# One 32-bit GpSimd addition that makes both pattern copies of a group, with a new order of the work

## The chip, the cores and the metric

The kernel runs on one core of one Trainium2 chip. The metric is the time of one execution in device microseconds. A time is given as the median of several runs. A profile shows one further execution, with every instruction of every engine: PE (TensorE), DVE (VectorE), ACT (ScalarE), POOL (GpSimd) and SP (SyncE, which issues most DMAs).

## The reference

Two independent attention blocks, A and B, each with S = 2048 tokens, D = 512 channels, 32 heads of 16 channels, in bfloat16. Block A is linear attention; block B is full softmax attention. Their outputs stand side by side in the result.

```python
# both: q, k, v = split((x @ wqkv)) into H = 32 heads of Dh = 16
# A
phi = lambda t: jnp.where(t > 0, t + 1, jnp.exp(t)) + 1e-6
kv = einsum("bhsd,bhse->bhde", phi(k), v); z = einsum("bhsd->bhd", phi(k))
o = einsum("bhqd,bhde->bhqe", phi(q), kv) / (einsum("bhqd,bhd->bhq", phi(q), z) + 1e-6)
a = merge_heads(o) @ wo
# B
p = softmax(einsum("bhqd,bhkd->bhqk", q, k) * Dh ** -0.5)
b = merge_heads(einsum("bhqk,bhkd->bhqd", p, v)) @ wo
return concatenate([a, b], axis=-1)
```

Most of the work is B's softmax: 32 heads x 2048 x 2048 scores, that is 2048 blocks of 128 keys by 512 queries.

## The kernel before, in words

**Blocks.** The scores of B are made transposed, in blocks of 128 keys (partitions) by 512 queries. A unit `u` is four heads and 512 queries; it has 16 x 4 = 64 blocks, and there are 32 units. For each block PE makes the scores (line 899: a matmul with 32 rows, four heads in the four row groups of the array), some engine makes the exponentials, and PE multiplies them by V with a column of ones (line 1306: 17 columns, four heads in the four column groups), summing into the one PSUM bank `pPV`. After a unit, DVE transposes the bank (line 1335), takes the reciprocal of the sums (line 1340), and POOL multiplies (line 1341).

**Two ways to an exponential.**
- ACT: one activation turns two or three blocks from the PSUM tile `pS` into f16 numbers in `PT` (line 1111).
- DVE and POOL: DVE scales a block from PSUM, adds a constant and writes it as a 16-bit integer into `DI` (line 1015). Read as f16, such a bit pattern is roughly the exponential, a straight line between powers of two. To make the error smaller, the sum of three patterns is used: the first, and two copies with a constant added to the integer (`SHIFT`, 328 and 656). PE multiplies each of the three by V: the first with `VX` (V scaled by `VW`), the two copies with `VV`. So such a block needs three PV matmuls and an ACT block one.

**Groups.** Two DVE blocks make a group (`DG = 2`), which lives in one of eight buffers of `DI` (`NDG = 8`). When both blocks are there, `chain` (line 1149) calls `shift` (line 1167) for copy 1 and copy 2. Each is either a POOL instruction (`on_pool`, lines 1174 to 1231) or, for copy 2 only and if POOL has much waiting (line 1239), a DVE instruction (`on_dve`, line 1170), which writes with a gap after every 32 numbers. In `DI` the eight first patterns stand together, then the eight copies 1, then the eight copies 2 (`di_at`). A POOL copy is a `tensor_scalar` on 16-bit integers, a multiplication by 1.0 and an addition. `on_pool` joins copies that are waiting: up to four copies of the same number from evenly spaced buffers in one instruction (line 1226), or one copy 1 and one copy 2 of different groups (line 1201; there copy 2 is made from copy 1).

**The order of the work** is planned in Python before anything runs. A list scheduler (lines 1575 to 1647) keeps a clock for each engine in `T` and candidates for each engine in `cands`, with a time at which they are ready, a priority and a price in us. It picks the earliest, and the run function of the pick emits instructions to that engine's queue. `Sched` turns reads and writes into semaphore waits. The prices are fixed: a POOL copy costs `PFX` = 0.272 us and 0.000834 us a pattern; `LPE["pool"]` (`PM` = -0.025) is the time from the end of a POOL instruction on that clock to its result being usable. `SEG` is a table with a row for each 12 us of PE's clock that sets 27 parameters of the planner, among them `PSH` and `DSH` (when DVE takes copy 2), `DBL` and `PBL` (how much may wait for DVE and POOL), `JN` (the longest join) and a seed for picks among near equals. So a change of a price or of a row reorders everything after it, and how many blocks go to ACT and how many to DVE comes out of the plan.

**Beside this** run block A (projections, line 609; `phi`, lines 721 to 724), B's projections and V (line 709 on DVE, and line 712 on POOL for `VX`), and the output projections, as jobs spread over the time.

Of the kernel before, what the change touches and what calls it, by code (L numbers as in the profile page):

```python
# [238 lines left out]
def bass_concat_heads__linear_attn_block__softmax_full_mha__prompt_kernel(nc, A_x, A_wqkv, A_wo, B_x, B_wqkv, B_wo, out):  # L239
# [89 lines left out]
    )  # L329
    GB = 0.0  # L330
    PM = -0.025
    JN = 4
    KSL = 0.02
    PFX = 0.272
# [33 lines left out]
    with es:  # L368
# [20 lines left out]

        def di_at(v, b):  # L390

            if v == 0:
                return b * (32 + DGW) + 32
            if v == 1:
                return NDG * (32 + DGW) + b * DGW
            return NDG * (32 + 2 * DGW) + b * ((DGW // 32) * 33 + 32)
# [120 lines left out]
        sch.add("pool", lambda e: e.memset(DI[:, 0:NDG * (32 + DGW)].rearrange("p (b n) -> p b n", b=NDG)[:, :, 0:32], 0.0), writes=[("DI", 2, b_) for b_ in range(NDG)])  # L517
        sch.add("pool", lambda e: e.memset(EA[:, 512:528], 0.0), writes=["EA"])
        for e_ in range(2):
            sch.add("dve", lambda e, e_=e_: e.tensor_reduce(PAR[:, e_:e_ + 1], ZMk[:].rearrange("p (a e) -> p e a", e=2)[:, e_, :],  # L520
                                                           axis=AX.X, op=ALU.max),
                    reads=["ZMk"], writes=[("PAR", e_)])
# [11 lines left out]
        LTO = {("pe", "dve"): 0.243, ("pe", "act"): 0.215, ("act", "dve"): 0.137, ("dve", "pool"): 0.166, ("pool", "dve"): -0.03, ("dve", "act"): 0.15}  # L534
# [165 lines left out]
        def v4_job(t4, Gp, **kw):  # L700
# [11 lines left out]
            st.append(("pool", 0.708, f_op("pool", lambda e: e.tensor_scalar(  # L712
# [436 lines left out]
        def chain(buf):  # L1149
# [17 lines left out]
            def shift(v, t_):  # L1167
                def on_dve(st_, en_):
                    wide = w + 32
                    sch.add("dve", lambda e: e.tensor_scalar(gapped(DI, di_at(v, buf), wide // 32, 32), DI[:, di_at(0, buf) - 32:di_at(0, buf) + w], 1.0, float(SHIFT[v - 1]),  # L1170
                                                             op0=ALU.mult, op1=ALU.add), reads=rk, writes=[("DI", v, buf)])
                    give(buf, v, "dve", en_)
# [71 lines left out]
            for v in (1, 2):  # L1244
                shift(v, s_["t"])
# [491 lines left out]
```

## Time and profile before

| | |
|---|---|
| median of 3 runs | 657.84 us (657.6 to 658.09) |
| the profiled execution's own time | 657.45 us |
| its span, first to last instruction | 655.7 us |
| chain that ended last, share of the span | DVE 45%, PE 32%, ACT 17%, POOL 3% |
| blocks on ACT, on DVE (PV matmuls from PT, from DI with VX) | 1355, 693 |
| pattern copies on POOL: instructions of lines 1226 and 1201 | 300 and 37 |
| pattern copies on DVE: instructions of line 1170 | 111 |

A row of a group of instructions has: line, engine, operation, output tile <- input tiles, shapes, count; then the busy time in us and the mean duration in ns; then the engine's idle time just before these instructions and what ended it. In the rows of stretches, each engine has its busy time and, in brackets, its number of instructions. Busy times of PE are modelled at their ends: a matmul of 512 columns shows 0.38 us though the next can follow sooner.

### The profile page before, as it was taken

Reading aid. Unit: us, or ns where it says so; the run is one execution under the profiler, and the core shown is the slowest. Engines: PE = TensorE matmul, PEld = TensorE weight load, DVE = VectorE, ACT = ScalarE, POOL = GpSimd, SP = SyncE. Lnnn points to the kernel's source line nnn. Section 1 sums busy time; section 2 is a strip of 40 time slices with the busy share of each in tenths; the row PEclk is TensorE's granted clock in tenths of the full one; section 3 lists DMA queues with packets and bytes.
Section 4 is the critical chain, followed back from the end, with each engine's and each line's share of the span. In section 5 each row is a group of like instructions: output and inputs, shape, how many; then the busy total and the mean of one; then the engine's idle time right before and its main releaser. Section 6 shows DMA issues by size and latency. Waiting matters only on the chain.

```text
span 655.7 us, 19281 instructions
## 1 busy us (share of the span) xinstructions
PE 639.1 (97%) x8321; PEld 215.3 (33%) x8322; DVE 633.4 (97%) x1101; ACT 641.4 (98%) x694; POOL 600.2 (92%) x418
## 2 busy tenths in 40 slices
PE   8999999999999999999999999999999999999995
PEld 5333433333333334322232223332323322232231
DVE  4999999999999999999999999999999999999984
ACT  6999999999999999999999999999999999999995
POOL 5999998999999999999999999999999999999994
PEclk9999999999999999999999999999999999999999
DMA  9701010111011103000210100100010010011111
GB/s 189 198 1 28 9 34 11 20 32 42 2 34 34 21 15 94 10 14 10 42 33 26 33 19 18 26 17 10 11 33 10 2 34 26 1 42 42 34 33 38
DMA packets 53227, 21.75 MB, mean 33 GB/s; under 512 B 44176, under 2 KB 52624, under 8 KB 53136
## 3 DMA queue, kind: packets, MB, share of 16 engines
q1 hardware_dynamic: 51664, 19.80, 13.2%
q8 instruction: 67, 1.10, 0.7%
q10 hardware_dynamic: 1472, 0.66, 0.4%
q14 instruction: 24, 0.20, 0.1%
HBM read 4.46 MB, written 4.19 MB: 13 GB/s over the span
## 4 chain that ended last, share of the span: by engine, by line
DVE 45%; PE 32%; ACT 17%; POOL 3%; DMA 1%; issue 1%; DVEq 0%; POOLq 0%
DVE DI L1015 30%; ACT PT L1111 17%; PE pPV L1306 11%; PE pS L899 11%; PE pD L609 6%; DVE DI L1170 5%; POOL DI L1226 2%; PE pS L609 2%; DVE OT L1335 1%; DVE KNa L724 1%; DVE VNa L764 1%; DVE VV L709 1%; DVE EC L722 1%; POOL DI L1201 1%; DMA xTb<-in_B_x_dram 1%
## 5 line engine op out<-in xcount | busy, mean ns | idle before, releaser
L1111 ACT ACTIVATE PT<-pS 128x1024 f16<-128x1024 f32 (+1 forms) x656 | 627.2, 1101 | 1.2 <-PE pS L899 1.0
L1226 POOL TENSOR_SCALAR DI<-DI 128x2048 int16<-128x2048 int16 (+2 forms) x300 | 491.6, 1639 | 33.7 <-DVE DI L1015 13.3
L1015 DVE TENSOR_SCALAR DI<-pD 128x512 int16<-128x512 f32 x505 | 330.6, 678 | 4.0 <-PE pD L899 2.4
L899 PE MATMUL pS<-QT,KM 32*128 32x512 bf16 x1543 | 260.4, 384 | 5.6 <-ACT PT L1111 4.7
L1306 PE MATMUL pPV<-PT,VV 128*17 128x512 f16 x1355 | 235.3, 381 | 0.0
L1306 PE MATMUL pPV<-DI,VV 128*17 128x512 f16 x1386 | 230.9, 383 | 0.7 <-DVE DI L1170 0.3
L899 PE MATMUL pD<-QT,KM 32*128 32x512 bf16 x505 | 181.2, 384 | 0.1
L1306 PE MATMUL pPV<-DI,VX 128*17 128x512 f16 x693 | 162.7, 381 | 0.7 <-DVE OT L1335 0.7
L899 PEld LDWEIGHTS pS<-QT,KM 32*128 32x128 bf16 x1543 | 65.2, 90 | 238.3 <-ACT PT L1111 183.8
L1015 DVE TENSOR_SCALAR DI<-pS 128x512 int16<-128x512 f32 x188 | 127.5, 678 | 0.1
L1170 DVE TENSOR_SCALAR DI<-DI 128x1056 int16<-128x1056 int16 x111 | 75.8, 690 | 0.3
L1201 POOL TENSOR_SCALAR DI<-DI 128x2048 int16<-128x2048 int16 x37 | 70.3, 1900 | 4.5 <-POOL DI L1226 1.8
L1306 PEld LDWEIGHTS pPV<-DI,VV 128*17 128x17 bf16 x1386 | 51.8, 88 | 50.2 <-issue 35.0
L1306 PEld LDWEIGHTS pPV<-PT,VV 128*17 128x17 bf16 x1355 | 53.9, 88 | 43.5 <-issue 32.0
L899 PEld LDWEIGHTS pD<-QT,KM 32*128 32x128 bf16 x505 | 43.4, 91 | 6.6 <-DVE DI L1015 4.6
L1306 PEld LDWEIGHTS pPV<-DI,VX 128*17 128x17 bf16 x693 | 37.1, 88 | 21.3 <-issue 13.0
L609 PE MATMUL pD<-Wa,xTa 128*32 128x256 bf16 x608 | 24.2, 275 | 0.3 <-DVE DI L1015 0.3
L609 PE MATMUL pD<-xTb,Wb 128*32 128x512 bf16 x304 | 23.9, 384 | 0.1
L1335 DVE STREAM_TRANSPOSE OT<-pPV 128x512 f32<-128x512 f32 x31 | 21.9, 706 | 0.0
L1341 POOL TENSOR_TENSOR OT<-OT,ZR 128x256 bf16<-128x256 f32 x31 | 19.3, 622 | 1.8
L609 PE MATMUL pS<-Wa,xTa 128*32 128x256 bf16 x416 | 16.9, 275 | 0.4 <-DVE DI L1015 0.4
L609 PEld LDWEIGHTS pD<-Wa,xTa 128*32 128x32 bf16 x608 | 13.2, 96 | 9.0 <-issue 5.3
(138 smaller groups left out, 384.9 us busy)
## 6 DMA issues: line engine op xcount, KB each, us to landing
out_dram<-KNa SPq DMA_DIRECT2D x31, 128.0 KB, 1.7
Wa<-in_A_wqkv_dram SPq DMA_DIRECT2D x1, 1536.0 KB, 8.3
KM<-KR SPq DMA_DIRECT2D x96, 16.0 KB, 1.8
Wb<-in_B_wqkv_dram SPq DMA_DIRECT2D x2, 384.0 KB, 4.8
Wb<-in_B_wqkv_dram SPq DMA_DIRECT2D x1, 512.0 KB, 4.7
Wa<-in_A_wo_dram SPq DMA_DIRECT2D x1, 512.0 KB, 4.6
Wa<-in_B_wo_dram SPq DMA_DIRECT2D x1, 512.0 KB, 4.4
ON<-in_B_x_dram ACTq DMA_DIRECT2D x1, 256.0 KB, 3.1
```

Source lines behind the costliest of these rows:

```text
L609: ins = self.e.matmul(out_[32 * g:32 * g + 32], lhsT=lhsT[:, 32 * g:32 * g + 32], rhs=rhs, start=start, stop=stop, tile_position=(0, 32 * g))
L709: st.append(("dve", 0.6, f_ev("dve", lambda e, bk: e.tensor_copy(VV[:, r, 4 * t4:4 * t4 + 4, :].rearrange("p t (h c) -> p t h c", c=17)[:, ...
L722: ("dve", 0.06 + n * 0.00054, f_op("dve", lambda e: e.tensor_scalar(gapped(EC, 0, n // 16 + 1, 16), EA[:, 0:n + 16], 1.0, 1e-6, op0=ALU.mi ...
L899: return e.matmul(dst, lhsT=KM[32 * g:32 * g + 32, Gp % 2, e_, j * 128:(j + 1) * 128], rhs=QT[32 * g:32 * g + 32, Gp % 2, c * 512:(c + 1) ...
L1015: sch.add("dve", lambda e: e.tensor_scalar(DI[:, di_at(0, buf) + i * 512:di_at(0, buf) + (i + n) * 512], f32v(DBANK[b0], n * 512), ESC, EB ...
L1111: sch.add("act", lambda e: e.activation(PTf[:, p0 * 512:p0 * 512 + w], S5[:, c0:c0 + w], ACTF.Exp, scale=SC), reads=skeys(sl, len(bl)), wr ...
L1170: sch.add("dve", lambda e: e.tensor_scalar(gapped(DI, di_at(v, buf), wide // 32, 32), DI[:, di_at(0, buf) - 32:di_at(0, buf) + w], 1.0, fl ...
L1201: sch.add("pool", lambda e: e.tensor_scalar(dv, sv, 1.0, float(SHIFT[0]), op0=ALU.mult, op1=ALU.add), reads=keys, writes=[("DI", v_, x) fo ...
L1226: sch.add("pool", lambda e: e.tensor_scalar(dv, sv, 1.0, sh_, op0=ALU.mult, op1=ALU.add), reads=keys, writes=[("DI", v, x) for x in best])
L1306: sch.add("pe", lambda e, g=g, j=j, c0=c0, V_=V_, r2=r2, P=P, first=first, last_=last_: e.matmul(PVb[32 * g:32 * g + 17, 0:512] if len(P.s ...
L1335: sch.add("dve", lambda e: e.transpose(OT[:, 0, :], PVb[:, 0:512]), reads=[("PV", g) for g in range(4)], writes=[("OT", 0)])
L1341: ("pool", 0.69, f_op("pool", lambda e: e.tensor_tensor(xn[:, :, 16 * e_:16 * e_ + 16], o[:, :, 0:16], zr.unsqueeze(2).broadcast_to([128, ...
```

## The change

Both copies of a group are made by one POOL `tensor_tensor` addition. `DI` is seen as 32-bit integers (`DW`), so one word holds two patterns; the other operand is a word of the new tile `CW`, whose two 16-bit halves both hold the number (328 in word 0, 656 in word 1), read again and again with step 0. The first patterns are read twice, with step 0 over the copies. For this the layout of `DI` changes: the first patterns, copy 1 and copy 2 of one buffer stand one after the other (`DIR` numbers a buffer). Where DVE makes copy 2, POOL's instruction makes copy 1 alone. Two neighbouring or evenly spaced groups can still be joined, as long as there are at most `JN` copies in all. The join of a copy 1 with another group's copy 2 is gone. The planner's prices change: `PFX`, `PM`, the latency from POOL to DVE, and the prices of two other POOL instructions. The rows of `SEG` are new.

```diff
-        (0.0,0.2,4,0.8,6,1,8,2,10.0,28,2.5,6.0,0.5,2.5,2,4.0,2.0,2.5,0.5,2,1,0.1,8,0,-9.0,4,2,6),
+        (0.0,0.3,4,5,0,0,8,2,9.5,36,2.5,6.0,1.8,1.8,2,7.0,2.0,3,1.5,1,1,0.1,4,0,-9.0,4,0.5,59),
...
-    PM = -0.025
+    PM = 0.097
-    PFX = 0.272
+    PFX = 0.144
...
+        DIR = 32 + 2 * DGW + (DGW // 32) * 33 + 32
+
         def di_at(v, b):
 
-            if v == 0:
-                return b * (32 + DGW) + 32
-            if v == 1:
-                return NDG * (32 + DGW) + b * DGW
-            return NDG * (32 + 2 * DGW) + b * ((DGW // 32) * 33 + 32)
+            return b * DIR + 32 + v * DGW
+        CW = sb("CW", [128, 2], mybir.dt.int32)
+        DW = DI.bitcast(mybir.dt.int32)
...
-        sch.add("pool", lambda e: e.memset(DI[:, 0:NDG * (32 + DGW)].rearrange("p (b n) -> p b n", b=NDG)[:, :, 0:32], 0.0), writes=[("DI", 2, b_) for b_ in range(NDG)])
+        sch.add("pool", lambda e: e.memset(DI[:, :].rearrange("p (b n) -> p b n", b=NDG)[:, :, 0:32], 0.0), writes=[("DI", 2, b_) for b_ in range(NDG)])
+        for v_ in range(2):
+            sch.add("pool", lambda e, v_=v_: e.memset(CW[:, v_:v_ + 1].bitcast(I16), float(SHIFT[v_])), writes=["CW"])
...
-        LTO = {("pe", "dve"): 0.243, ("pe", "act"): 0.215, ("act", "dve"): 0.137, ("dve", "pool"): 0.166, ("pool", "dve"): -0.03, ("dve", "act"): 0.15}
+        LTO = {("pe", "dve"): 0.243, ("pe", "act"): 0.215, ("act", "dve"): 0.137, ("dve", "pool"): 0.166, ("pool", "dve"): 0.07, ("dve", "act"): 0.15}
...
-            st.append(("pool", 0.708, f_op("pool", lambda e: e.tensor_scalar(
+            st.append(("pool", 0.61, f_op("pool", lambda e: e.tensor_scalar(
...
-            def shift(v, t_):
-                def on_dve(st_, en_):
...
-                def on_pool(st_, en_):
...
+            def on_pool(st_, en_):
+                near_ = {x[1]: x for x in pshift if x[0] == vs and x[2] == w and x[3][0] <= st_ + PMW}
+                near_[buf] = me[0]
+                best = [buf]
+                for step in range(1, NDG):
+                    run_ = [buf]
+                    while (len(run_) + 1) * len(vs) <= JN and run_[-1] + step in near_:
+                        run_.append(run_[-1] + step)
+                    while (len(run_) + 1) * len(vs) <= JN and run_[0] - step in near_:
+                        run_.insert(0, run_[0] - step)
+                    if len(run_) > len(best):
+                        best = run_
...
+                T["pool"] = en_ = st_ + PFX + len(best) * len(vs) * w * 0.000833
+                gs = [(best[1] - best[0]) * DIR // 2 if len(best) > 1 else 1, len(best)]
+                part = lambda t_: list(t_[:, 0:1].ap[0])
+                dv = bass.AP(DW, DW[:, di_at(vs[0], best[0]) // 2:].offset, [part(DW), gs, [DGW // 2, len(vs)], [1, w // 2]])
+                sv = bass.AP(DW, DW[:, di_at(0, best[0]) // 2:].offset, [part(DW), gs, [0, len(vs)], [1, w // 2]])
+                cv = bass.AP(CW, CW[:, vs[0] - 1:].offset, [part(CW), [0, len(best)], [1, len(vs)], [0, w // 2]])
+                sch.add("pool", lambda e: e.tensor_tensor(dv, sv, cv, op=ALU.add), reads=keys + ["CW"], writes=[("DI", v, x) for v in vs for x in best])
...
+            vs = (1, 2)
+            if late:
+                for v in vs:
+                    push("dve", s_["t"], -2, 0.06 + w * 0.00027, plain(v))
+                return
+            if p_backlog(s_["t"]) - DSH * d_backlog(s_["t"]) > PSH:
+                vs = (1,)
+                push("dve", s_["t"], 1, 0.06 + (w + 32) * 0.00053, on_dve)
+            for v in vs:
+                pv_give[buf, v] = lambda en_, v=v: give(buf, v, "pool", en_)
+            me = [(vs, buf, w, push("pool", s_["t"] + LTO["dve", "pool"], 0, PFX + len(vs) * w * 0.000833, on_pool), rk)]
+            pshift.append(me[0])
...
-                  ("pool", 0.69, f_op("pool", lambda e: e.tensor_tensor(xn[:, :, 16 * e_:16 * e_ + 16], o[:, :, 0:16],
+                  ("pool", 0.59, f_op("pool", lambda e: e.tensor_tensor(xn[:, :, 16 * e_:16 * e_ + 16], o[:, :, 0:16],
```

More of the change, by code (lines that the diff above doesn't have):

```diff
@@ L1165, in give @@
                     pv_ready[b[0]].append((en_ + (LPE["pool"] if lane == "pool" else LPE["dve"]), b, (P, ("DI", v, buf_)), ("d", buf_), "V"))
-            def shift(v, t_):
-                def on_dve(st_, en_):
[L1169 to L1172, printed above, removed]
-                def on_pool(st_, en_):
-                    near_ = {x[1]: x for x in pshift if x[0] == v and x[2] == w and x[3][0] <= st_ + PMW}
-                    best = [buf]
-                    for step in range(1, NDG):
-                        run_ = [buf]
-                        while len(run_) < JN and run_[-1] + step in near_:
-                            run_.append(run_[-1] + step)
-                        while len(run_) < JN and run_[0] - step in near_:
-                            run_.insert(0, run_[0] - step)
-                        if len(run_) > len(best):
-                            best = run_
-                    d1 = lambda b_: dgroup["st"][b_].get("v1", 1e9)
-                    two = [x for x in pshift if x[2] == w and x[1] != buf and x[0] != v and x[3][0] <= st_ + PMW
-                           and d1(x[1] if v == 1 else buf) <= st_]
-                    if len(best) == 1 and two:
-                        o = min(two, key=lambda x: x[3][2])
-                        pshift.remove(me[0])
-                        pshift.remove(o)
-                        cands["pool"].remove(o[3])
-                        segs = sorted([(buf, v), (o[1], o[0])])
-                        st_ = max(st_, o[3][0], d1(o[1] if v == 1 else buf) + 0.05)
-                        keys = []
-                        for b_, v_ in segs:
-                            keys += [("DI", 1, b_)] if v_ == 2 else [("DI", 0, b_, i) for i in range(n)]
-                        T["pool"] = en_ = st_ + PFX + 2 * w * 0.000834
-                        moves = sorted((di_at(v_ - 1, b_), di_at(v_, b_)) for b_, v_ in segs)
-                        sv, dv = [bass.AP(DI, DI[:, x[0]:x[0] + 1].offset, [list(DI[:, 0:w].ap[0]), [x[1] - x[0], 2], [1, w]]) for x in zip(*moves)]
-                        sch.add("pool", lambda e: e.tensor_scalar(dv, sv, 1.0, float(SHIFT[0]), op0=ALU.mult, op1=ALU.add),
-                                reads=keys, writes=[("DI", v_, x) for x, v_ in segs])
-                        for x, v_ in segs:
-                            if v_ == 1:
-                                dgroup["st"][x]["v1"] = en_
-                            pv_give[x, v_](en_)
-                        return
-                    keys = []
-                    for b_ in best:
-                        x = near_.get(b_, me[0])
-                        pshift.remove(x)
-                        if b_ != buf:
-                            cands["pool"].remove(x[3])
-                            st_ = max(st_, x[3][0])
-                        keys += [("DI", 0, b_, i) for i in range(n)]
-                    T["pool"] = en_ = st_ + PFX + len(best) * w * 0.000834
-                    moves = [(di_at(0, b_), di_at(v, b_)) for b_ in best]
-                    def view(offs):
-                        one = DI[:, offs[0]:offs[0] + w]
-                        if len(offs) == 1:
-                            return one
-                        return bass.AP(one.tensor, one.offset, [list(one.ap[0]), [offs[1] - offs[0], len(offs)], [1, w]])
-                    sv, dv = view([m_[0] for m_ in moves]), view([m_[1] for m_ in moves])
-                    sh_ = float(SHIFT[v - 1])
-                    sch.add("pool", lambda e: e.tensor_scalar(dv, sv, 1.0, sh_, op0=ALU.mult, op1=ALU.add),
-                            reads=keys, writes=[("DI", v, x) for x in best])
-                    for x in best:
-                        if v == 1:
-                            dgroup["st"][x]["v1"] = en_
-                        pv_give[x, v](en_)
-                pv_give[buf, v] = lambda en_: give(buf, v, "pool", en_)
-                if late:
-                    def plain(st_, en_):
-                        sch.add("dve", lambda e: e.tensor_scalar(DI[:, di_at(v, buf):di_at(v, buf) + w], DI[:, di_at(0, buf):di_at(0, buf) + w], 1.0, float(SHIFT[v - 1]), op0=ALU.mult, op1=ALU.add),
-                                reads=rk, writes=[("DI", v, buf)])
-                        give(buf, v, "plain", en_)
-                    push("dve", t_, -2, 0.06 + w * 0.00027, plain)
-                elif v == 2 and p_backlog(t_) - DSH * d_backlog(t_) > PSH:
-                    push("dve", t_, 1, 0.06 + (w + 32) * 0.00053, on_dve)
-                else:
-                    me = [(v, buf, w, push("pool", t_ + LTO["dve", "pool"], 0, PFX + w * 0.000834, on_pool), rk)]
-                    pshift.append(me[0])
@@ L1244, in chain, with on_dve, plain, run @@
-            for v in (1, 2):
-                shift(v, s_["t"])
+            def on_dve(st_, en_):
+                wide = w + 32
+                sch.add("dve", lambda e: e.tensor_scalar(gapped(DI, di_at(2, buf), wide // 32, 32), DI[:, di_at(0, buf) - 32:di_at(0, buf) + w], 1.0, float(SHIFT[1]),
+                                                         op0=ALU.mult, op1=ALU.add), reads=rk, writes=[("DI", 2, buf)])
+                give(buf, 2, "dve", en_)
+            def plain(v):
+                def run(st_, en_):
+                    sch.add("dve", lambda e: e.tensor_scalar(DI[:, di_at(v, buf):di_at(v, buf) + w], DI[:, di_at(0, buf):di_at(0, buf) + w], 1.0, float(SHIFT[v - 1]), op0=ALU.mult, op1=ALU.add),
+                            reads=rk, writes=[("DI", v, buf)])
+                    give(buf, v, "plain", en_)
+                return run
@@ new lines, in on_pool @@
+            def on_pool(st_, en_):
[10 more added lines that the diff above has]
+                        best = run_
+                keys = []
+                for b_ in best:
+                    x = near_[b_]
+                    pshift.remove(x)
+                    if b_ != buf:
+                        cands["pool"].remove(x[3])
+                        st_ = max(st_, x[3][0])
+                    keys += [("DI", 0, b_, i) for i in range(n)]
+                T["pool"] = en_ = st_ + PFX + len(best) * len(vs) * w * 0.000833
[5 more added lines that the diff above has]
+                sch.add("pool", lambda e: e.tensor_tensor(dv, sv, cv, op=ALU.add), reads=keys + ["CW"], writes=[("DI", v, x) for v in vs for x in best])
+                for x in best:
+                    for v in vs:
+                        pv_give[x, v](en_)
@@ new lines, in chain @@
+            vs = (1, 2)
[6 more added lines that the diff above has]
+                push("dve", s_["t"], 1, 0.06 + (w + 32) * 0.00053, on_dve)
+            for v in vs:
+                pv_give[buf, v] = lambda en_, v=v: give(buf, v, "pool", en_)
+            me = [(vs, buf, w, push("pool", s_["t"] + LTO["dve", "pool"], 0, PFX + len(vs) * w * 0.000833, on_pool), rk)]
```

106 rows, old and new, of the table SEG are left out of this document.

## The prediction

> **What bounds the kernel now.** I read the page first, then the busy time of three stretches (start, middle, end). Columns of the second fence: length of the stretch, then busy time and number of instructions of PE, PEld, DVE, ACT and POOL, granted clock, DMA share, GB/s.
>
> ```profile
> span 655.7 us, 19281 instructions
> PE 639.1 (97%) x8321; PEld 215.3 (33%) x8322; DVE 633.4 (97%) x1101; ACT 641.4 (98%) x694; POOL 600.2 (92%) x418
> ```
> ```profile
> 0.00:12.00 12.00, 9.45 (x105) 7.25 (x106) 4.99 (x15) 5.91 (x7) 7.72 (x27) 1.00 0.93 199
> 12.00:640.00 628.00, 620.24 (x8152) 205.28 (x8149) 621.34 (x1073) 627.80 (x681) 585.49 (x382) 1.00 0.13 30
> 640.00:656.00 16.00, 9.38 (x71) 2.81 (x72) 7.12 (x14) 7.66 (x9) 7.04 (x10) 0.91 0.13 38
> ```
>
> No single engine bounds it. In the middle 628 us ACT is busy for 627.80, so the span is start plus ACT's exponentials plus end: it gets shorter only if ACT has fewer blocks. PE has 7.76 us idle there, DVE 6.66. POOL shows 42.5 us idle, but part of that is not usable, as its rows show below. The granted clock is 1.00, so no term hangs on it.
>
> What passes between the engines is blocks of 128x512 scores. Next, the groups of instructions:
>
> ```profile
> L1111 ACT ACTIVATE PT<-pS 128x1024 f16<-128x1024 f32 (+1 forms) x656 | 627.2, 1101 | 1.2 <-PE pS L899 1.0
> L1306 PE MATMUL pPV<-PT,VV 128*17 128x512 f16 x1355 | 235.3, 381 | 0.0
> L1306 PE MATMUL pPV<-DI,VX 128*17 128x512 f16 x693 | 162.7, 381 | 0.7 <-DVE OT L1335 0.7
> ```
> ```profile
> L1015 DVE TENSOR_SCALAR DI<-pD 128x512 int16<-128x512 f32 x505 | 330.6, 678 | 4.0 <-PE pD L899 2.4 <-PE pS L899 0.7
> L1015 DVE TENSOR_SCALAR DI<-pS 128x512 int16<-128x512 f32 x188 | 127.5, 678 | 0.1
> L1170 DVE TENSOR_SCALAR DI<-DI 128x1056 int16<-128x1056 int16 x111 | 75.8, 690 | 0.3
> ```
>
> 1355 blocks have one PV matmul from PT: ACT made them. 693 have one from DI with VX: DVE made them; 2048 together. An ACT block costs ACT 627.2 / 1355 = 0.463 us. A DVE block costs DVE (330.6 + 127.5) / 693 = 0.661 us, two more PV matmuls on PE (three patterns instead of one), and two pattern copies. Two blocks make a group, so a copy of a group is 1024 patterns, and there are as many such copies as blocks, 693: DVE makes 111 of them (L1170, 0.690 us each), POOL the other 582.
>
> **POOL, before.** Its groups by shape, its longest waits, and two places of its timeline (start, duration):
>
> ```profile
> L1226 POOL TENSOR_SCALAR DI<-DI 128x2048 int16<-128x2048 int16 x177 | 336.4, 1901 | 20.3 <-DVE DI L1015 9.0
> L1226 POOL TENSOR_SCALAR DI<-DI 128x1024 int16<-128x1024 int16 x105 | 109.9, 1047 | 11.3 <-DVE DI L1015 3.7
> L1201 POOL TENSOR_SCALAR DI<-DI 128x2048 int16<-128x2048 int16 x37 | 70.3, 1900 | 4.5 <-POOL DI L1226 1.8 <-DVE DI L1015 0.6 <-DVE VNa L764 0.2
> L1226 POOL TENSOR_SCALAR DI<-DI 128x3072 int16<-128x3072 int16 x16 | 44.1, 2753 | 2.0 <-DVE DI L1015 0.6 <-DVE RHA L774 0.3
> L1341 POOL TENSOR_TENSOR OT<-OT,ZR 128x256 bf16<-128x256 f32 x31 | 19.3, 622 | 1.8
> L1226 POOL TENSOR_SCALAR DI<-DI 128x512 int16<-128x512 int16 x2 | 1.2, 621 | 0.2
> L1398 POOL TENSOR_TENSOR OT<-OT,ZR 128x128 bf16<-128x128 f32 x2 | 0.8, 402 | 0.9 <-DVE ZR L1397 0.9
> L518 POOL MEMSET EA<- 128x16 bf16 x1 | 0.1, 112 | 0.0
> ```
> ```profile
> POOL DI L1226 <- DVE DI L1015: 13.3, 35, 1.4
> POOL VX L712 <- DVE VV L709: 5.5, 4, 4.2
> ```
> ```profile
> 316.72 0.62 POOL L1341 TENSOR_TENSOR OT<-OT,ZR 128x256 bf16<-128x256 f32 x1
> 317.41 12.07 POOL L1226 TENSOR_SCALAR DI<-DI 128x2048 int16<-128x2048 int16 x7
> ...
> 336.70 0.62 POOL L1341 TENSOR_TENSOR OT<-OT,ZR 128x256 bf16<-128x256 f32 x1
> 337.29 3.88 POOL L1226 TENSOR_SCALAR DI<-DI 128x2048 int16<-128x2048 int16 x2
> ```
>
> From 1024 to 2048 patterns the duration rises by 854 ns, from 2048 to 3072 by 852: 0.834 ns a pattern and 193 ns fixed. Two in a row take 3.88 us, that is 2 x 1.90 and 0.08 between them. So an instruction occupies POOL for 0.272 us plus 0.854 a copy: 337 x 0.272 + 582 x 0.854 = 91.7 + 497.0 = 588.7 us. All the rest of POOL (other work, start, end, waits, of which the two rows above are 18.8) is 655.7 - 588.7 = 67 us.
>
> **What the change removes and adds on POOL.** The 337 TENSOR_SCALAR go; each group gets one TENSOR_TENSOR on 32-bit words, for both copies, or for one where DVE takes the other. Two groups can still be joined (four copies at most). For 582 copies that is between 146 instructions (always four) and 346 (one a group, no joins); I take 300, since joins need neighbouring buffers to be ready together, and before they reached only 582 / 337 = 1.7 copies.
>
> The price of one is not in the trace; the nearest rows are the TENSOR_TENSOR with a broadcast operand, L1341 and L1398. From 128 to 256 elements they rise by 220 ns: 1.72 ns an element, 182 ns fixed. A word carries two patterns, so a pattern would cost 0.86 ns, against 0.834: the word form wins nothing by size. Lower bound: 0.834 ns a pattern, the row of the one-input form. Upper bound: L1341 with no fixed share at all, 622 / 256 = 2.43 ns a word. I take the slope halfway between 0.834 and 0.86, 0.867 us a copy, since both rows nearly agree.
>
> The Trainium skill ("GPSIMD Engine Reference", section 3.1) speaks against the change here: it gives a two-input add on GpSimd about 2.6 cycles an element against about one for one input, and 4497 ns for 2048 of 32 bits, 2.2 ns an element. By that, a copy would cost 512 x 2.2 = 1.13 us (an estimate from that page). L1341 with 1.72 ns stands between, nearer to the change's side; no row has 32-bit integers.
>
> So the gain must come from the fixed part. It has two bounds: L1341 at 336.70 ends at 337.32 and its successor starts at 337.29, 0.03 earlier; the one at 316.72 ends at 317.34 and its successor starts at 317.41, 0.07 later. So 0.182 becomes 0.15 or 0.25 us an instruction. I take 0.15, because a TENSOR_TENSOR has both kinds of successor and the new planner prices (0.144, and 0.59 for L1341) put the order on the early one; the late one is a rival. For the same 582 copies: 300 x 0.15 + 582 x 0.867 = 45 + 505 = 550 us, 39 less than 588.7. Bounds: 70 if every end is the good one (146 x 0.15 + 497 = 519), 2 with the late handoff and 0.88 us a copy (75 + 512 = 587).
>
> **What 39 us of POOL are worth.** The new order has to turn them into fewer ACT blocks. For 1 us less of the span:
> - ACT must lose 1 / 0.463 = 2.16 blocks.
> - DVE must make them (2.16 x 0.661 = 1.43) and be 1 us shorter too: 2.43 us, which is 2.43 / 0.690 = 3.5 copies handed to POOL.
> - POOL takes 3.5 + 2.16 copies of 0.94 us (0.867 and half of 0.15), and is 1 us shorter: 6.3 us.
> So POOL allows 39 / 6.3 = 6.2 us. PE is asked for 2.16 x 2 more matmuls. Its pieces in the chain of work (start, duration):
>
> ```profile
> 308.20 0.55 PE pPV L1306 x8
> 315.40 0.76 PE pPV L1306 x12
> 322.43 0.97 PE pPV L1306 x16
> ```
> ```profile
> 120.00:180.00 60.00, 59.95 (x917) 21.36 (x909) 59.79 (x107) 60.00 (x67) 55.84 (x35) 1.00 0.14 26
> PE pPV L1306 <- POOL DI L1226: 0.2, 1, 0.2
> ```
>
> Four more matmuls cost 0.21 us, so 4.3 cost 0.23: each microsecond gained asks PE for 1.23. It has 7.76 us idle in the middle; the stretch 120 to 180 shows that idle can sink to 0.05 in 60, so some 0.5 stays: (7.76 - 0.5) / 1.23 = 5.9 us. PE binds a little before POOL; I take 5.9. DVE then makes 13 blocks more (706), POOL 616 copies, and L1170 falls by 21 to about 90.
>
> **Terms at nothing.** The two memsets of the constant and the zeroing over all rows: L518 costs 0.11 us, ahead of the first scores in a stretch where POOL is busy 7.72 of 12; uncovered they would cost 0.3. The new layout of DI moves no work. The first copy of a group now comes with the second, at 1.9 us instead of 1.05: behind it stand PV matmuls, which the order does last; before, PE stood idle for POOL's copies once, for 0.2 us. If that cover were gone, at most the 0.85 us would show, at the end of the work, where it cannot be reordered; POOL's next instruction waits for nothing new, since the copies of a group had the same inputs before. The DVE plain copies at the end have no row before; none is expected.
>
> **Sum.** The profiled execution took 657.45 us, its span 655.7, so 1.75 lie around it; the median of the three runs shown is 657.84, 0.4 above it. 657.45 - 5.9 = 651.55, and by the median 651.9: I say 652.
>
> **Rivals.**
> - *PE pays less than I think* (faster still). Both copies of a group arrive together, which fills rounds of four better: 1386 + 693 matmuls in full rounds of 0.21. If PE gives way, POOL's upper end is the limit, 70 / 6.3 = 11 us: 646 to 649. For: POOL's idle; against: PE's 59.95 of 60. Chance 0.14.
> - *The freed POOL time isn't converted* (no change). ACT is already at 627.80 of 628 and PE near full; if PE's idle is the price of changing between kinds of matmul, more DVE blocks only press on PE and 0 to 1.3 us are won: 656.5 to 659. Chance 0.12.
> - *The late handoff* (slower). If the word addition is followed 0.07 us late, as at 316.72, the fixed part is 0.25 and the order, laid out for 0.15, sends POOL 616 copies: 616 x 0.867 + 300 x 0.25 = 609; with the 67 of the rest and the 1.75 around the span 678, and with the 18.8 of waits gone 659. In the middle 668. It decides from a fixed part of about 0.24 us on (534 + 300 x 0.24 + 67 - 18.8 = 654, next to the span of 655.7). For: the one-input instructions all stand 0.08 apart; against: 336.70. Chance 0.10.
> - *The word costs more* (much slower). At L1341's upper bound, 2.43 ns, 616 copies of 512 words cost 766 us, and with the 67 of the rest the span would be 833. As the 1.72 ns row stands against it, chance 0.04. By the 2.2 ns of the Trainium skill ("GPSIMD Engine Reference", section 3.1) it would be about 800, an estimate from that page.
> That the order does not do what it says (two copies an instruction) is not possible by the diff: the second copy has no other path but L1170's.
>
> **How the numbers follow.** My forecast (649 to 656.5, 652 the likeliest) has 0.60; with the first rival faster is 0.74. A run of this kernel can be told from no change at about 0.2%, 1.3 us. Same 0.12, slower 0.14. The range goes from 646 (the first rival's end) to 660, past no change; it leaves out the two costly rivals but for their near end, and a little below.
>
> **What would show it.** In the profile after: a POOL TENSOR_TENSOR group DI<-DI,CW whose 2048 patterns (1024 words) take 1.85 to 1.95 us; its successor starting at its end or before; some 300 of them against 337; L1170 near 90; DVE blocks (VX matmuls) near 706; ACT's L1111 near 621 us; PE idle in the middle near 1 us. I am wrong if the word form takes over 2.1 us for 2048 patterns, if successors stand 0.07 apart, or if PE's idle stays near 8 us with POOL clearly under 90%.

## The result, and the profile after

The kernel after takes 651.27 us (median of 4 runs, 650.7 to 651.69) against 657.82 us (4 runs, 657.6 to 658.09): a ratio of 0.990, 95% interval 0.9883 to 0.9917. That is 6.55 us less; 5.9 were forecast. The profiled execution took 651.69 us, its span 649.9.

From the page and its three stretches (columns as before):

```profile
span 649.9 us, 19218 instructions
PE 637.8 (98%) x8355; PEld 214.4 (33%) x8356; DVE 622.5 (96%) x1080; ACT 633.5 (97%) x689; POOL 616.8 (95%) x347
ACT 66%; PE 16%; DVE 16%; DMA 1%; issue 0%; SPq 0%
```
```profile
0.00:12.00 12.00, 9.71 (x97) 7.45 (x98) 4.99 (x15) 5.45 (x7) 7.79 (x29) 1.00 0.87 189
12.00:640.00 628.00, 623.20 (x8227) 204.97 (x8228) 613.64 (x1056) 626.88 (x681) 608.23 (x316) 1.00 0.13 30
640.00:656.00 16.00, 4.94 (x43) 2.01 (x32) 3.89 (x9) 1.19 (x2) 0.81 (x2) 0.89 0.16 54
```

In the middle ACT is as full as before, 626.88 of 628 us; POOL is busier (608.23 us, before 585.49), and DVE is idle for 14.36 us, before 6.66. The gain stands in the last stretch, which ends 5.8 us sooner, because ACT had less to do in all. The third line of the page is the chain that ended last: two thirds of it are ACT now. The blocks:

```profile
L1113 ACT ACTIVATE PT<-pS 128x1024 f16<-128x1024 f32 (+1 forms) x651 | 619.4, 1096 | 1.9 <-PE pS L901 1.0
L1284 PE MATMUL pPV<-PT,VV 128*17 128x512 f16 x1338 | 232.6, 381 | 0.0
L1284 PE MATMUL pPV<-DI,VX 128*17 128x512 f16 x710 | 162.8, 381 | 0.4 <-DVE OT L1313 0.4
```
```profile
L1171 DVE TENSOR_SCALAR DI<-DI 128x1056 int16<-128x1056 int16 x73 | 49.8, 687 | 0.2
L1177 DVE TENSOR_SCALAR DI<-DI 128x1024 int16<-128x1024 int16 x4 | 1.5, 424 | 0.1
```

17 blocks went from ACT to DVE (1355 to 1338, 693 to 710), and 38 copies from DVE to POOL (111 to 73). Four more copies are made by DVE in a plain form (L1177), which the kernel before did not use. POOL by shape, and two places of its timeline:

```profile
L1208 POOL TENSOR_TENSOR DI<-DI,CW 128x2048 int32<-128x2048 int32 x79 | 283.4, 3600 | 1.7 <-DVE DI L1017 0.5
L1208 POOL TENSOR_TENSOR DI<-DI,CW 128x1024 int32<-128x1024 int32 x132 | 246.9, 1892 | 4.1 <-DVE DI L1017 3.8
L1208 POOL TENSOR_TENSOR DI<-DI,CW 128x512 int32<-128x512 int32 x53 | 55.0, 1039 | 0.0
```
```profile
314.92 0.62 POOL L1319 TENSOR_TENSOR OT<-OT,ZR 128x256 bf16<-128x256 f32 x1
315.50 17.26 POOL L1208 TENSOR_TENSOR DI<-DI,CW 128x2048 int32<-128x2048 int32 x7
...
324.60 8.15 POOL L1208 TENSOR_TENSOR DI<-DI,CW 128x2048 int32<-128x2048 int32 x3
332.71 0.62 POOL L1319 TENSOR_TENSOR OT<-OT,ZR 128x256 bf16<-128x256 f32 x1
333.30 1.04 POOL L1208 TENSOR_TENSOR DI<-DI,CW 128x512 int32<-128x512 int32 x1
```

264 instructions carry 79 x 4 + 132 x 2 + 53 = 633 copies. From 1024 to 2048 words the duration rises by 1708 ns, 1.668 ns a word, so a copy of 512 words costs 0.854 us as before, and 0.184 us is fixed. A successor that waits for nothing starts 0.04 us before its predecessor's end (314.92 + 0.62 against 315.50; 324.60 + 8.15 against 332.71). So an instruction occupies POOL for 0.142 us plus 0.854 a copy: 264 x 0.142 + 633 x 0.854 = 37 + 541 = 578 us, 10 less than the 588.7 of before for 51 copies more. The rest of POOL is 649.9 - 578 = 72 us.

### The profile page after: what moved, and what is told of

Its sections match the earlier page's. It is cut to its first block, busy times and chain, and to the rows that moved or that the text cites. A ratio compares the mean times of both kernels' runs of the same rounds, so it can differ in the third digit from the quotient of the medians.

```text
span 649.9 us, 19218 instructions
## 1 busy us (share of the span) xinstructions
PE 637.8 (98%) x8355; PEld 214.4 (33%) x8356; DVE 622.5 (96%) x1080; ACT 633.5 (97%) x689; POOL 616.8 (95%) x347
## 3 DMA queue, kind: packets, MB, share of 16 engines
q1 hardware_dynamic: 51664, 19.80, 13.3%
## 4 chain that ended last, share of the span: by engine, by line
ACT 66%; PE 16%; DVE 16%; DMA 1%; issue 0%; SPq 0%
ACT PT L1113 65%; DVE DI L1017 11%; PE pPV L1284 5%; PE pS L901 5%; PE pD L611 2%; ACT EA L723 1%; PE pS L611 1%; DVE DI L1171 1%; DMA xTb<-in_B_x_dram 1%; DVE PQT L726 1%; DVE VNa L813 1%; DVE KNa L597 0%; DVE OT L1313 0%; PE pS L1336 0%; PE pD L901 0%; DMA KNa<-VNa 0%
## 5 line engine op out<-in xcount | busy, mean ns | idle before, releaser
L1113 ACT ACTIVATE PT<-pS 128x1024 f16<-128x1024 f32 (+1 forms) x651 | 619.4, 1096 | 1.9 <-PE pS L901 1.0
L1208 POOL TENSOR_TENSOR DI<-DI,CW 128x1024 int32<-128x1024 int32 (+2 forms) x264 | 580.7, 2232 | 5.8 <-DVE DI L1017 4.3
L1017 DVE TENSOR_SCALAR DI<-pD 128x512 int16<-128x512 f32 x512 | 336.9, 682 | 5.7 <-PE pD L901 3.9
L1284 PE MATMUL pPV<-PT,VV 128*17 128x512 f16 x1338 | 232.6, 381 | 0.0
L901 PE MATMUL pD<-QT,KM 32*128 32x512 bf16 x516 | 185.7, 384 | 0.5 <-DVE DI L1017 0.4
L1017 DVE TENSOR_SCALAR DI<-pS 128x512 int16<-128x512 f32 x194 | 131.5, 678 | 0.3 <-PE pS L901 0.3
L1284 PEld LDWEIGHTS pPV<-DI,VV 128*17 128x17 bf16 x1420 | 49.5, 88 | 45.0 <-issue 33.6
L1171 DVE TENSOR_SCALAR DI<-DI 128x1056 int16<-128x1056 int16 x73 | 49.8, 687 | 0.2
L597 DVE CAST KNa<-pD 128x512 bf16<-128x512 f32 x21 | 14.3, 681 | 3.1 <-PE pD L611 3.1
L714 POOL TENSOR_SCALAR VX<-VV 128x544 bf16<-128x544 bf16 x16 | 10.2, 646 | 6.5 <-DVE VV L711 6.5
```

Of the source, the lines that this page charges most:

```text
L597: return lambda e, bk: (e.tensor_copy(out_fn(), in_fn(bk)) if lane == "dve" else e.activation(out_fn(), in_fn(bk), ACTF.Copy))
L714: st.append(("pool", 0.61, f_op("pool", lambda e: e.tensor_scalar(VX[:, r, 4 * t4:4 * t4 + 4, :].rearrange("p t c -> p (t c)"), VV[:, r, 4 ...
L901: return e.matmul(dst, lhsT=KM[32 * g:32 * g + 32, Gp % 2, e_, j * 128:(j + 1) * 128], rhs=QT[32 * g:32 * g + 32, Gp % 2, c * 512:(c + 1) ...
L1017: sch.add("dve", lambda e: e.tensor_scalar(DI[:, di_at(0, buf) + i * 512:di_at(0, buf) + (i + n) * 512], f32v(DBANK[b0], n * 512), ESC, EB ...
L1113: sch.add("act", lambda e: e.activation(PTf[:, p0 * 512:p0 * 512 + w], S5[:, c0:c0 + w], ACTF.Exp, scale=SC), reads=skeys(sl, len(bl)), wr ...
L1171: sch.add("dve", lambda e: e.tensor_scalar(gapped(DI, di_at(2, buf), wide // 32, 32), DI[:, di_at(0, buf) - 32:di_at(0, buf) + w], 1.0, fl ...
```

## The experiments

A handoff is the gap from the end of one POOL instruction to the start of the next. I call it late at 0.06 to 0.08 us and early at about -0.04.

My theory: a copy costs the same, the fixed part falls, POOL is thereby able to take more, and the new order turns this into fewer ACT blocks. Rivals: the order alone made the gain; POOL's time was spare; and the early handoff comes from the new layout of DI, not from the instruction.

**The layout alone** (layout16), the kernel before with

```diff
+        DIR = 32 + 2 * DGW + (DGW // 32) * 33 + 32
...
-            if v == 0:
-                return b * (32 + DGW) + 32
-            if v == 1:
-                return NDG * (32 + DGW) + b * DGW
-            return NDG * (32 + 2 * DGW) + b * ((DGW // 32) * 33 + 32)
+            return b * DIR + 32 + v * DGW
...
```

> The kernel before with one edit: DI laid out as in the kernel after (first patterns, copy 1 and copy 2 of a buffer one behind the other). Same order, same 16-bit additions. Theory place (the late handoff of 0.08 us comes from where copy 1 stands): the successors of the copies start 0.03 to 0.04 us early instead of 0.08 late, so 337 instructions give back about 40 us of POOL; the order is the old one, so POOL only waits longer for DVE (13 us before) and the time stays between 656 and 658. Theory kind (the late handoff belongs to the 16-bit TENSOR_SCALAR): handoffs stay at 0.08 and nothing changes, 657.8.

Measured: 657.75 us against 657.77, ratio 0.9996 (0.9986 to 1.0006). Its POOL timeline still has 3.88 us for two of 1.90:

```profile
367.96 3.88 POOL L1224 TENSOR_SCALAR DI<-DI 128x2048 int16<-128x2048 int16 x2 [0.52 <-DVE DI L1013]
```

The late handoff stays: it is not the place.

**The word addition with the copies elsewhere** (sep), the kernel after with

```diff
-            return b * DIR + 32 + v * DGW
+            return b * (32 + DGW) + 32 if v == 0 else NDG * (32 + DGW) + b * DIC + (v - 1) * DGW
...
```

> The kernel after with one edit: the first patterns stand in a region of their own, the two copies of a buffer in pairs behind it. Same order, same word additions. Theory place: handoffs become late (0.07 instead of -0.04), 264 x 0.11 = 29 us more of POOL, which has 20 us idle in the middle: slower, 655 to 670. Theory kind: handoffs stay early, 651.3 as after.

Measured: 651.77 us, ratio to the kernel before 0.9908 (0.9892 to 0.9925).

```profile
314.67 0.62 POOL L1320 TENSOR_TENSOR OT<-OT,ZR 128x256 bf16<-128x256 f32 x1
315.25 17.25 POOL L1209 TENSOR_TENSOR DI<-DI,CW 128x2048 int32<-128x2048 int32 x7
332.46 0.62 POOL L1320 TENSOR_TENSOR OT<-OT,ZR 128x256 bf16<-128x256 f32 x1
```

The handoffs stay early (314.67 + 0.62 against 315.25; 315.25 + 17.25 against 332.46), save where POOL waits for something. Place is ruled out from both sides.

**The new order with 16-bit additions** (two16), the kernel after with

```diff
-                sch.add("pool", lambda e: e.tensor_tensor(dv, sv, cv, op=ALU.add), reads=keys + ["CW"], ...)
+                for v in vs:
+                    sch.add("pool", lambda e, d16=d16, s16=s16, v=v: e.tensor_scalar(d16, s16, 1.0, float(SHIFT[v - 1]), op0=ALU.mult, op1=ALU.add), ...)
```

> The kernel after, same order and layout, but each word addition is replaced by 16-bit TENSOR_SCALAR additions, one for each copy number (joined groups stay joined): 264 + 211 = 475 instructions for the same 633 copies. My theory (a copy costs 0.854 us either way, the gain is the fixed part): theory place gives 475 x 0.15 + 541 = 612 us of POOL against 578 after; with the other 72 of POOL less up to 22 of waits the span is 662 to 684. Theory kind gives 475 x 0.272 + 541 = 670, a span of 720 to 742. Rival (POOL is not what limits, the order alone made the gain): under 655.

Measured: 730.95 us (one run), span 729.2. Its chain and POOL groups:

```profile
POOL 60%; DVE 20%; PE 15%; issue 4%; ACT 1%; DMA 1%; DVEq 0%
L1212 POOL TENSOR_SCALAR DI<-DI 128x2048 int16<-128x2048 int16 x168 | 318.8, 1898 | 13.3
L1212 POOL TENSOR_SCALAR DI<-DI 128x1024 int16<-128x1024 int16 x297 | 310.3, 1045 | 24.4 <-DVE DI L1017 1.4
PE pPV L1289 <- POOL DI L1212: 38.5, 64, 1.6
```

There are 465 additions, not the 475 expected, because ten of the joined instructions hold the copy 1 of two groups and no copy 2. The durations by size are the old ones. There are only more instructions, 0.06 to 0.08 us lie between any two additions, and PE now waits 38.5 us for copies. So the new order does not pay with the old instruction as it was, with 328 and 656.

**A little more of the fixed part** (pad), the kernel after with

```diff
...
+                sch.add("pool", lambda e: e.memset(PD[:, pd, :], 0.0), writes=[("PD", pd)])
                 sch.add("pool", lambda e: e.tensor_tensor(dv, sv, cv, op=ALU.add), ...)
```

> The kernel after with a small memset of a spare tile ahead of each of the 264 word additions, worth about 0.095 us of POOL each, 25 us in all: it brings the fixed part of 0.142 us near 0.24, the point from which the late handoff was to decide. Mine: POOL's sum is 578 + 25 + 72 = 675 less up to 22 of waits: span 653 to 675, about 660. Rival (the freed POOL time is spare, ACT alone limits): 651 to 652.

Measured: 669.71 us (669.21 to 671.1), ratio to the kernel before 1.0186 (1.0169 to 1.0203); span 667.4. Stretch, chain, wait and timeline:

```profile
12.00:640.00 628.00, 613.00 (x7973) 198.69 (x7969) 605.30 (x1032) 614.46 (x666) 622.41 (x569) 1.00 0.12 28
POOL 86%; PE 8%; DVE 4%; DMA 1%; ACT 0%; issue 0%
POOL DI L1213 <- DVE DI L1019: 2.7, 4, 1.3
...
304.14 1.90 POOL L1213 TENSOR_TENSOR DI<-DI,CW 128x1024 int32<-128x1024 int32 x1
305.97 0.16 POOL L1212 MEMSET PD<- 128x64 bf16 x1
306.07 1.90 POOL L1213 TENSOR_TENSOR DI<-DI,CW 128x1024 int32<-128x1024 int32 x1
```

From one addition to the next it is 306.07 - 304.14 = 1.93 us, where 1.89 - 0.04 = 1.85 stood in the kernel after: 0.08 more, 264 x 0.08 = 21 us. The time rises by 18.4 us, ACT falls to 614.46 busy of 628, and POOL makes 86% of the chain. So POOL's time is not spare in the new order: of 21 us more on POOL, 18.4 show in the end.

**The word addition in the old order** (word_oldorder), the kernel before with

```diff
-                    sch.add("pool", lambda e: e.tensor_scalar(dv, sv, 1.0, sh_, op0=ALU.mult, op1=ALU.add),
-                            reads=keys, writes=[("DI", v, x) for x in best])
+                    sch.add("pool", lambda e: e.tensor_tensor(dv, sv, cv, op=ALU.add),
+                            reads=keys + ["CW"], writes=[("DI", v, x) for x in best])
...
```

> The kernel before, same order and layout, with each of its 337 16-bit additions on POOL replaced one for one by a word addition (same groups, same copy, same place in the order). Mine: a copy still costs 0.854 us, the handoff becomes early, 337 x 0.12 = 40 us of POOL are freed, but the blocks are shared out as before, 1355 to ACT, so the time stays at 656.5 to 658.5 and POOL only waits more for DVE (15 us before, some 50 now). Rival (POOL's lateness held up the old order): 650 to 655 without any new order.

Measured: 657.53 us against 657.69, ratio 0.9996 (0.9986 to 1.0005).

```profile
12.00:640.00 628.00, 620.21 (x8152) 205.04 (x8149) 621.35 (x1073) 627.80 (x681) 574.21 (x382) 1.00 0.13 30
POOL DI L1235 <- DVE DI L1019: 41.5, 86, 1.5
```

POOL is busy for 574.21 instead of 585.49 us and waits 41.5 us for DVE instead of 13.3; ACT has its 627.80 as before. Freed POOL time without a new order is worth nothing.

**Which number is added** (one_const), the kernel before with

```diff
-                    sh_ = float(SHIFT[v - 1])
+                    sh_ = float(SHIFT[1])
...
-                        sch.add("pool", lambda e: e.tensor_scalar(dv, sv, 1.0, float(SHIFT[0]), op0=ALU.mult, op1=ALU.add),
+                        sch.add("pool", lambda e: e.tensor_scalar(dv, sv, 1.0, float(SHIFT[1]), op0=ALU.mult, op1=ALU.add),
```

In the trace of before, every handoff below 0.1 us with a copy 1 on one side is late (290 of them). Those between a copy 2 and line 1341 are early, but for four in which line 1341 waited for DVE's reciprocal. Copy 1 adds 328 and copy 2 adds 656 (the joined instructions of line 1201 hold a copy 1 and add 328), so that trace alone can't tell the copy from the number.

> The kernel before, but every 16-bit addition on POOL adds 656; before, those that make a copy 1 added 328, so POOL's copies 1 have another number in them and the sums are others. Theory constant (the late handoff goes with the number 328): all handoffs between copies become 0.04 early instead of 0.08 late, time 656.5 to 658.5. Theory copy (it goes with copy 1, whatever the number): they stay at 0.08, 657.8.

Measured: 657.37 us (one run). The first line is from the kernel before, the others from this run; two instructions of 1.90 us now take 3.76 instead of 3.88:

```profile
366.54 3.88 POOL L1226 TENSOR_SCALAR DI<-DI 128x2048 int16<-128x2048 int16 x2 [0.52 <-DVE DI L1015]
366.52 3.76 POOL L1226 TENSOR_SCALAR DI<-DI 128x2048 int16<-128x2048 int16 x2 [0.89 <-DVE DI L1015]
POOL DI L1226 <- DVE DI L1015: 38.5, 80, 1.5
```

The handoff goes with the number: with 656 everywhere it is early (3.76 - 2 x 1.90 = -0.04), save where POOL waits for something, and POOL waits 38.5 us for DVE, as with the word addition.

**More numbers** (numbers): copies 2 add 656, copies 1 sixteen numbers in turn.

> The kernel before, same order, but POOL's copies 2 all add 656 and its copies 1 add in turn 328, 320, 324, 327, 329, 336, 352, 384, 256, 164, 300, 512, 640, 1312, 2 and 655, so its patterns, and the sums, are others. It asks which numbers bring the late handoff. If it hangs on the size, all numbers up to some limit between 328 and 656 are late; if 328 is special by its digits, some of the smaller ones are early. The time is not the point: 657 to 658.

Measured: 657.58 us (one run). At one place, where the two additions add 656 and 512, the kernel before (first line) has 3.88 us and this run 3.76:

```profile
385.90 3.88 POOL L1226 TENSOR_SCALAR DI<-DI 128x2048 int16<-128x2048 int16 x2
385.88 3.76 POOL L1231 TENSOR_SCALAR DI<-DI 128x2048 int16<-128x2048 int16 x2
```

Beside a 656, and leaving out longer waits, 164, 300, 320, 324, 327, 328, 329, 336, 352 and 1312 have the late handoff (0.06 to 0.08 us) in every case. 2, 256, 384, 512, 640 and 655 have the early one (-0.04), but for seven of 0.08: in six of them a joined instruction (line 1203 there) waits for the copy 1 that POOL has only just made, and in one, at 384, POOL waits for DVE. It isn't size: 164 and 1312 are late, 2 and 640 early. Why these numbers and not those stays open.

**Orders made with equal effort** (old_rowA, new_rowB): both kernels with one row of SEG for the whole time, for each the row of the two tables with which the planner's own clock ends first.

```diff
+        (0.0,0.3,4,3.0,0,1,6,2,10.0,36,2.5,6.0,1.2,2.5,2,7.0,2.0,2.5,1.5,1,1,0.3,4,0,-9.0,4,0.5,180),
...
+        (0.0,0.05,5,3,4,1,6,2,9.5,32,2.5,9.0,0.8,2.5,2,7.0,1.5,2.5,0.5,1,1,0.3,6,10,-9.0,4,0,14),
```

> The kernel before with one row of the planner's table for the whole time, the row (of all that the two tables hold) with which its own clock ends first. It shows the kernel before without the search row by row: 5 to 10 us slower than before, 662 to 668.

> The kernel after with one row for the whole time, again the one with which its own clock ends first. Theory instruction (the word addition is worth some 6 us whatever the search): 5 to 9 us faster than the kernel before with its best single row. Theory search (the gain is the longer search of rows): no faster than that one, 662 to 668.

Measured: 663.89 us (1.0091, 1.0069 to 1.0112) and 656.40 us (0.9979, 0.9968 to 0.9989). They are 7.5 us apart without any search row by row (6.1 by the spans of the profiled executions, 661.0 and 654.9), and 6.55 with it (5.8 by the spans): the gain belongs to the instruction and its prices, given an order made for them.

**Each part without the other's order** (op_oldseg: the kernel after with the old table; seg_only: the kernel before with the new table).

```diff
-        (0.0,0.3,4,5,0,0,8,2,9.5,36,2.5,6.0,1.8,1.8,2,7.0,2.0,3,1.5,1,1,0.1,4,0,-9.0,4,0.5,59),
+        (0.0,0.2,4,0.8,6,1,8,2,10.0,28,2.5,6.0,0.5,2.5,2,4.0,2.0,2.5,0.5,2,1,0.1,8,0,-9.0,4,2,6),
...
```

> The kernel after (word additions, new prices) with the planner's table of the kernel before: the change without its new order. If the word addition pays by itself under any order: 651 to 655. Mine, after the one-row runs: a row acts through a chain of picks, so an old table is as good as a random one for the new prices; it loses the whole search, 5 to 15 us, more than the 6 it gains: 656 to 675, slower than the kernel before.

> The kernel before (16-bit additions, old prices) with the new table: the new order's parameters without the new instruction. If the gain lay in better rows as such: below 656. Mine: it loses the search made for it and gains nothing, 660 to 670.

Measured: 676.07 us (1.0274, 1.024 to 1.0308), a little past my range, and 663.84 us (1.0088, 1.0053 to 1.0123). In op_oldseg's middle:

```profile
12.00:640.00 628.00, 618.89 (x7959) 208.01 (x7956) 578.11 (x988) 618.64 (x666) 591.28 (x320) 1.00 0.13 28
POOL DI L1208 <- DVE DI L1017: 29.4, 30, 5.7
```

ACT itself has 9.4 us idle there and DVE 50: this order, made for other prices, loses more than the instruction gains. Which of its picks cost the most the runs don't show.

**A further search of the table** (searched): 51 of 54 rows changed.

```diff
-        (12.0,0.05,5,3,4,1,6,3,9.5,26,2.5,9.0,0.5,1.8,2,7.0,2.0,2.5,1.5,1,1,0.3,6,10,-9.0,4,0,182),
+        (12.0,0.05,5,3,4,1,6,3,9.5,26,2.5,9.0,0.5,1.8,2,7.0,2.0,2.5,1.5,1,1,0.3,6,10,-9.0,8,0,55),
...
```

> The kernel after with nothing but other rows in the planner's table (51 of 54 changed, joins of up to eight copies allowed in some), found by further picks that let the planner's own clock end some 2 us sooner. POOL still had 20 us idle and DVE 14 in the middle of the kernel after. Mine: the measured time follows the planner's clock, 648.5 to 650.5, with more copies on POOL and PE's idle below 4 us. Rival (the order is at its limit, ACT and PE leave no room): 651 to 652.

Measured: 651.77 us (651.04 to 652.02), ratio to the kernel before 0.9903 (0.9887 to 0.992): past my range, and no better than the kernel after.

```profile
span 648.7 us, 19228 instructions
12.00:640.00 628.00, 623.18 (x8238) 204.20 (x8236) 613.02 (x1052) 626.68 (x682) 615.94 (x321) 1.00 0.13 30
```

Its span is 1.2 us shorter, but 3.3 us instead of 1.8 lie around it (652.02 - 648.7), and 3.3 to 3.8 in its other runs. What fills them the profile doesn't show; old_rowA has 3.1. So it stays open whether the order is at its limit. PE's idle is as in the kernel after.

## Why the prediction was right

- **What bounds it**: as put. ACT had 627.80 of 628 and has 626.88; its exponentials fell from 627.2 to 619.4 us, and word_oldorder shows that nothing moves while they stay.
- **The price of a copy**: 0.867 us taken, 0.854 measured, the lower bound. The Trainium skill ("GPSIMD Engine Reference", section 3.1) gives 4497 ns for a two-input fp32 addition of 2048 elements. The 2.2 ns an element, an estimate from that figure, does not hold for this int32 addition with a repeated operand: 1.668 ns a word were measured.
- **The fixed part**: 0.15 taken, 0.142 measured. The value was nearly right, but one of its two reasons was wrong. I took the two handoffs beside line 1341 for two kinds of successor of a TENSOR_TENSOR. They hung on the number in the neighbouring 16-bit addition (328 at 317.41, 656 at 337.29), which the word addition reads from a tile. What was left was the hint in the planner's new prices.
- **Where the fixed part went**: with early handoffs the 337 instructions of before would have cost 337 x (0.193 - 0.036) = 53 us of the 91.7, and the 264 of after cost 37. So up to 39 us come from the handoff and some 15 from there being fewer. The 39 is an upper value, because the sum gives all 337 a late handoff, also those that waited for DVE anyway; in word_oldorder POOL's waits for DVE rose by 28 us (13.3 to 41.5). Putting both copies in one instruction is the smaller part for POOL. A rival stays untested: 16-bit additions with two numbers of the early kind, under an order made for them. So the runs show that the word addition brings the gain, not that it is the only way to it.
- **The counts**: 300 instructions and 616 copies forecast, 264 and 633 measured. At the measured prices 36 instructions fewer save 5 us and 17 copies more cost 15. POOL's sum still came out (578 us, and 616 x 0.867 + 300 x 0.15 = 579 by the forecast), because the price of a copy was put a little too high. L1170 at 90, now L1171 at 73; 706 blocks, 710 measured; ACT 621, 619.4 measured.
- **PE** was mis-sized: "PE binds a little before POOL". A microsecond was to ask 1.23 of PE's idle, which was to fall from 7.76 to about 1; it fell to 4.80. Over the span PE is busy 637.8 us against 639.1, though it has 34 PV matmuls more. So PE gave way in part, as the first rival had it. The traces hold about as many stretches of PV matmuls as before (446, now 448), and more of them are a multiple of four long (332, now 346). That fits fuller rounds, but no run tests it.
- **What a microsecond costs** was mis-sized too, and here the near hit is in good part luck. For the same 582 copies the change freed 588.7 - (264 x 0.142 + 497) = 54 us of POOL, not 39. At 6.3 us for each microsecond, that allowed 8.6 us, more than the 6.2 of the forecast. But the span fell by 5.8, so one cost 54 / 5.8 = 9.3. ACT had to lose 17 blocks, not 13, since its time outside the exponentials rose from 28.5 us (655.7 - 627.2) to 30.5 (649.9 - 619.4). DVE handed over 38 copies, not 21, and did not use all the time that this freed: its idle in the middle rose from 6.66 to 14.36 us. Too little freed and too low a price cancel, and the bound of PE, from which the 5.9 came, was not reached.
- **The late handoff**, the slower rival, did not come, but pad puts its price on the chip: at 0.142 + 0.08 = 0.22 the span is 667.4. I had put the turning point at 0.24, with a rest of 67 - 18.8 = 48 us; in pad the rest is 667.4 - (541 + 264 x 0.22) = 68. The waits for DVE's blocks did go (13.3 to 2.7 us), but those of `VX` stayed (5.5, now 5.8), and POOL's last addition now starts 22 us before the end of the span (645.7 of 667.4), where it was 10 before (645.8 of 655.7). In the kernel after it is 22 as well (627.9 of 649.9). With a rest of 68 to 72 the sum reaches 655.7 at a fixed part of 0.16 to 0.18, an estimate from these runs: the change had far less room than I gave it.
- **Terms at nothing**: of DVE's plain copies "none is expected", and there are four, 1.5 us in all, behind POOL's last addition. The two memsets of the constant take 0.2 us.
- **The order**: I took it as given that the new order would fit. op_oldseg shows what hung on it, 25 us.

## What to carry to other kernels

Where four engines are full together, freed time on one is worth nothing until blocks are shared out anew; test an instruction and the order made for it together, and compare with the old instruction under an order made with the same effort. Before a change of instruction, look at the gaps between neighbours as well as at durations: here up to 39 of 54 us lay in a gap. Idle time counts as room only where the engine has work left to do: here POOL's waits for DVE went, but the stretch behind its last addition grew from 10 to 22 us.

## What the runs showed of the hardware

The gap between two POOL instructions hangs on the number in a 16-bit TENSOR_SCALAR: 0.08 us beside one that adds 328, -0.04 beside one that adds 656, with the same place, size and order and where POOL waits for nothing. Changing the number alone let POOL be done sooner with the same work: its waits for DVE rose from 13.3 to 38.5 us, at the same time of the kernel. A two-operand addition of 32-bit integers with the second operand repeated cost 1.668 ns a word on POOL, twice the 0.834 ns of a one-input 16-bit element: by the pattern, the same.
